# Spectral filter and feed-forward kernel: rows normalised ahead of the first stage, W mirrored by a gather, the row mean kept out of the residual, the d-transform cut by lo positions, and a new table of the order

## Chip, cores and metric

One core of a Trainium2 chip. The metric is the device time of one execution in microseconds (us). The engines are TensorE (PE; PEld is its weight load), VectorE (DVE), ScalarE (ACT), GpSimd (POOL) and SyncE (SP, which here only issues transfers).

## The reference

Two rounds of a spectral block A and a feed-forward block B on x of 2048 positions (s) by 448 features (d), bf16:

```python
def _A_ref(x, w_r, w_i):
    X = rfft2(x.astype(float32), axes=(-2, -1))
    return irfft2(X * (w_r + 1j * w_i), (S, D), axes=(-2, -1)).astype(bfloat16)

def _B_ref(x, w1, b1, w2, b2):
    h = einsum("bsd,df->bsf", x, w1) + b1
    r = where(h > 0, h, 0)
    return einsum("bsf,fd->bsd", r * r, w2) + b2

x = x + _A_ref(_layernorm(x), A_w_r, A_w_i)
x = x + _B_ref(_layernorm(x), B_w1, B_b1, B_w2, B_b2)
x = x + _A_ref(_layernorm(x), A_w_r, A_w_i)
x = x + _B_ref(_layernorm(x), B_w1, B_b1, B_w2, B_b2)
```

S is 2048, D 448, the hidden width 1792; w_r and w_i have 2048 x 225 entries. The layernorm has no weights, only a mean and a standard deviation of each row.

## The kernel before

**Tiles.** x lies in SBUF as 16 tiles (t) of 128 rows. The transform over s is split: partition and tile give 16 coarse positions (hi) and 128 fine ones (lo). Frequencies go in pairs p = 1 to 7 and a special item p = 0.

**Spectral block.** Stage A (`first_A`, L803, and `second_A`, L1175) transforms over hi, tile by tile, into `XA`. Stage TD (`stage_TD`, L860) transforms over d into `U`, two components for each pair. Stage B (`stage_B`, L877) transforms over lo with the constants `G_sb` into `EF`. Stage W (`stage_W`, L910) multiplies by the filter on DVE: each pair needs rows of W and their mirror image. Stage Bi (L949) goes back over lo (matmuls with `H_sb` or `HS_sb`) into `VT`, TI (L980) back over d into `TIo`, AI (L994) back over hi, with the residual added on DVE (L1030). In the first round stage A takes `xin` and a reversed copy `xr` as weights, matrix `FA` scaled by the row's 1/std (`Fs`, made on POOL), and a further matmul with `m2`, minus twice the row mean. The mirror image of W is made by matmuls with the reversal matrix `J_sb` (`w_mirror`, L761).

**Feed-forward block.** `ln_B` (L1049) makes the statistics: the residual operation sums a row on DVE as it writes, ACT sums its squares, DVE forms the variance (`u`), ACT takes the root. Tiles 0 to 3 are not normalised: their mean and std go as extra columns through the first product, against column sums of W1 that `w1_aux` (L743) makes by matmuls and small transfers. Tiles 0 and 1 are transposed on TensorE (`flip`, L1036), the others by DMA transposes on SP. Then `h_part` or `h_pairs` (first product; a relu on ACT, a square on DVE), then `o_tile` (second product; the residual on DVE, with `xb` = x + b2 ready beforehand). Behind each `o_tile` of the first round, DVE makes the statistics and sums for the second spectral block, tile by tile (tags A2.t).

**Order.** `_Sched` records all operations and then places them: at each step it takes, among the units that may start, by priority: the length of the chain behind a unit plus a bias out of `PR` and a table `ADJ` by tag. It also chooses between ACT and DVE for evacuations, picks the PSUM banks, and puts warm-up matmuls (`ones`, L1278) where it expects TensorE to be idle. Each engine then runs its list in order and waits on semaphores.

Of the kernel before, what the change touches and what calls it, by code (L numbers as in the profile page):

```python
# [10 lines left out]
P = 128  # L11
S = 2048
# [3 lines left out]
NFS = 6  # L16
NT = 16
# [8 lines left out]
H_PAIRS = tuple(p for p in range(1, 8) if p not in SD_PAIRS)  # L26

# [9 lines left out]
def make_constants():  # L37
# [20 lines left out]
    dd = np.arange(HD)[:, None]  # L58
    l = np.arange(1, 225)[None, :]
    th = 2 * np.pi * l * (dd - 223.5) / D  # L60
    TD = np.zeros((2, 2, P, LW))
    for g, M in enumerate((np.cos(th), -np.sin(th))):
        TD[g, 0] = M[:P]
        TD[g, 1, 32:] = M[P:]
# [11 lines left out]
    lo = (m % 8) * 16 + m // 8  # L76
    k2 = np.arange(P)
    kk = [0, 8, 1, 2, 3, 4, 5, 6, 7]
    G = np.zeros((P, 9, 3, P))
    H = np.zeros((P, 9, 2, 2 * P))  # L80
    for i, k1 in enumerate(kk):
        th = 2 * np.pi * lo[:, None] * (k1 + 16 * k2[None, :]) / float(S)
        G[:, i, 0] = np.cos(th)
        G[:, i, 1] = -np.sin(th)
        G[:, i, 2] = np.sin(th)
# [16 lines left out]
    for g, M in enumerate((cl * np.cos(th), cl * np.sin(th))):  # L102
        for r in range(2):
            TI[:, r, g] = M[r::2]

    HS = np.stack([np.stack([-H[:, p + 1, 1], H[:, p + 1, 0], H[:, p + 1, 1], -H[:, p + 1, 0]], 1) for p in range(1, 8)], 1)
# [5 lines left out]

PR = {'A1': 65800.0, 'A1step': 7500.0, 'TD': [48800.0, -113100.0], 'B': [36300.0, -23900.0], 'W': [76300.0, 35800.0], 'Bi': [21700.0, 28400.0], 'step': [16400.0, 1100.0], 'M': 33500.0, 'aux': -104400.0, 'ramp': [210200.0, 192900.0], 'rstep': [2800.0, 6700.0], 'late': [85200.0, 100700.0], 'lstep': [5400.0, 6200.0], 'TI': [53500.0, 42800.0], 'AI': [44600.0, 400.0], 'h': [57700.0, -6500.0], 'A2': -27100.0, 'xb': 113100.0}
ADJ = {"": -1463273, "A1.0": 1085981, "A1.1": 710040, "A1.2": 717802, "A1.3": 364623, "A1.4": 440691, "A1.5": 740255,
# [68 lines left out]
class _Unit:  # L183


    def __init__(self, eng, rows=128):
        self.eng = eng
        self.ops = []
        self.tiles = []
        self.rows = rows  # L190
        self.prio = 0.0
        self.bias = 0.0
        self.seq = 0
        self.tag = ""
# [1162 lines left out]
```

## Time and profile before

| what | us |
|---|---|
| runs, median of 3 (lowest, highest) | 273.26 (272.47, 273.49) |
| profiled execution, span | 271.4 |
| first matmul of stage A starts | 9.12 |
| last matmul of the first Bi ends (about) | 44.8 |
| first feed-forward's first h matmul starts | 52.29 |
| second d-transform starts | 148.16 |
| second feed-forward's first h matmul starts | 178.32 |
| last matmul ends | 268.9 |

The span goes from the first to the last instruction of the profiled execution; the runs are timed from outside, so what lies around the span is in their time and not in it. The page gives no time of its own for the profiled execution besides the span.

In the profile's rows "out<-in" names what an operation writes and reads. A row of the timeline begins with its start and its length in us; "[0.71 <-DVE ...]" behind it is idle time of the engine just before, and who ended it. Most matmuls have the one line L622 and most DVE operations L676, those of helper functions, so the names tell them apart: `Fs,tmp` is the second stage A, `TD_sb,XA` the d-transform, `arena,G_sb` stage B, `HS_sb` and `H_sb` stage Bi, `TI_sb,VT` and `tmp,FI_sb` the way back, `J_sb,x_sb` the flips, `yT,W_sb` and `yT,VT` the first product, `W_sb,arena` the second.

### The profile page before, as it was taken

How to read it: one execution, taken by the hardware profiler on the slowest of the kernel's cores; microseconds unless marked ns; L12 is line 12 of the kernel's file. 1: busy time of each engine (PE TensorE's matmuls, PEld its weight loads, DVE VectorE, ACT ScalarE, POOL GpSimd, SP SyncE). 2: the span in 40 equal slices, each digit the busy share in tenths (PEclk: the TensorE clock that was granted, in tenths of full speed). 3: DMA queues.
4: the chain of work that ended last, by engine and by line, in shares of the span. 5: the costliest groups of instructions: out<-in, count | busy, mean ns of one | idle time of the engine just before them, and what ended most of it. 6: DMA issues, size and time to landing. Idle time of an engine off the chain costs nothing.

```text
span 271.4 us, 5706 instructions
## 1 busy us (share of the span) xinstructions
PE 260.9 (96%) x2086; PEld 159.0 (59%) x2086; DVE 206.8 (76%) x730; ACT 179.4 (66%) x382; POOL 13.3 (5%) x28
## 2 busy tenths in 40 slices
PE   7899988999999999999998999988999999999996
PEld 2588736786744554445557775776764454454554
DVE  4878994999999999457996998398998654556122
ACT  2698986997849728786206897897667833787000
POOL 4860000000000000000000000000000000000000
DMA  7999800004203123000000000004242023200101
GB/s 254 341 382 304 215 14 2 2 4 77 61 14 41 32 46 70 2 1 2 0 0 2 2 0 1 2 1 42 56 97 68 0 66 81 41 0 2 51 34 51
DMA packets 28566, 16.71 MB, mean 62 GB/s; under 512 B 21838, under 2 KB 27194, under 8 KB 28412
## 3 DMA queue, kind: packets, MB, share of 16 engines
q1 hardware_dynamic: 28108, 15.62, 22.5%
q10 hardware_dynamic: 432, 0.75, 0.8%
q8 instruction: 16, 0.26, 0.4%
q14 instruction: 10, 0.08, 0.1%
HBM read 10.85 MB, written 1.84 MB: 47 GB/s over the span
## 4 chain that ended last, share of the span: by engine, by line
PE 77%; DVE 13%; DMA 3%; ACT 3%; issue 2%; POOL 0%; ACTq 0%; DVEq 0%
PE ps L622 77%; DVE tmp L676 6%; DVE arena L676 3%; DMA yT<-x_sb 2%; DVE st L777 1%; ACT tmp L647 1%; DMA xin<-in_A_x_dram 1%; ACT VT L1054 1%; ACT VT L647 0%; DVE VT L676 0%; DVE x_sb L1171 0%; PE ps L1278 0%; ACT mv L641 0%; DVE yT L648 0%; DVE Fs L659 0%
## 5 line engine op out<-in xcount | busy, mean ns | idle before, releaser
L622 PE MATMUL ps<-yT,W_sb 64*128 64x512 bf16 (+1 forms) x770 | 89.5, 346 | 1.0 <-DMA yT<-x_sb 0.7
L622 PE MATMUL ps<-W_sb,arena 128*128 128x448 bf16 (+1 forms) x476 | 86.6, 341 | 0.0
L622 PEld LDWEIGHTS ps<-yT,W_sb 64*128 64x128 bf16 (+1 forms) x770 | 50.6, 95 | 38.6 <-DMA yT<-x_sb 1.1
L622 PEld LDWEIGHTS ps<-W_sb,arena 128*128 128x128 bf16 x476 | 46.2, 98 | 37.3 <-DVE arena L676 0.4
L676 DVE TENSOR_TENSOR arena<-arena 128x512 bf16<-128x512 bf16 (+1 forms) x140 | 49.5, 369 | 21.9 <-ACT arena L641 21.6
L641 ACT ACTIVATE arena<-ps,b1col 128x512 bf16<-128x512 f32 x84 | 52.5, 686 | 12.8 <-PE ps L622 12.6
L1171 DVE SCALAR_TENSOR_TENSOR x_sb<-ps,arena 128x448 bf16<-128x448 f32 (+1 forms) x26 | 15.3, 587 | 17.3 <-PE ps L622 16.8
L647 ACT ACTIVATE arena<-ps 128x896 bf16<-128x896 f32 (+1 forms) x37 | 24.8, 784 | 2.2 <-PE ps L622 2.1
L641 ACT ACTIVATE mv<-mv,epst 128x2 f32<-128x2 f32 (+1 forms) x38 | 11.1, 295 | 20.8 <-DVE mv L778 15.7
L647 ACT ACTIVATE XA<-ps 128x512 bf16<-128x512 f32 x32 | 17.8, 603 | 6.7 <-PE ps L622 6.7
L641 ACT ACTIVATE arena<-ps 128x256 bf16<-128x256 f32 x56 | 19.1, 406 | 4.4 <-PE ps L622 3.4
L647 ACT ACTIVATE VT<-ps 128x512 bf16<-128x512 f32 (+1 forms) x32 | 17.9, 626 | 5.0 <-PE ps L622 5.0
L1054 ACT ACTIVATE VT<-x_sb 128x448 bf16<-128x448 bf16 x32 | 18.4, 580 | 3.8 <-DVE x_sb L1030 3.8
L622 PE MATMUL ps<-yT,VT 64*128 64x512 bf16 x42 | 15.8, 376 | 0.0
L622 PE MATMUL ps<-HS_sb,arena 128*128 128x512 bf16 x64 | 14.9, 380 | 0.7 <-DVE arena L676 0.6
L647 ACT ACTIVATE tmp<-ps 128x896 bf16<-128x896 f32 (+1 forms) x18 | 14.0, 849 | 2.2 <-PE ps L622 2.2
L668 ACT ACTIVATE arena<-x_sb,mv,rstd 128x448 bf16<-128x448 bf16 x11 | 8.3, 759 | 10.4 <-DMA yT<-arena 7.8
L622 PE MATMUL ps<-arena,G_sb 128*128 128x448 bf16 (+1 forms) x72 | 13.6, 332 | 0.0
L622 PE MATMUL ps<-TD_sb,XA 112*128 112x112 bf16 (+1 forms) x184 | 13.4, 229 | 0.0
L622 PEld LDWEIGHTS ps<-TD_sb,XA 112*128 112x128 bf16 (+1 forms) x184 | 12.2, 98 | 1.6 <-ACT XA L647 0.5
L676 DVE TENSOR_TENSOR VT<-tmp 128x448 bf16<-128x448 bf16 x24 | 8.8, 384 | 4.4 <-ACT tmp L647 4.4
L1030 DVE SCALAR_TENSOR_TENSOR x_sb<-ps,xin 128x448 bf16<-128x448 f32 x16 | 9.5, 620 | 3.3 <-PE ps L622 3.3
(81 smaller groups left out, 309.2 us busy)
## 6 DMA issues: line engine op xcount, KB each, us to landing
out_dram<-x_sb SPq DMA_DIRECT2D x15, 112.0 KB, 1.7
W_sb<-in_B_w_dram SPq DMA_DIRECT2D x1, 1568.0 KB, 15.6
W_sb<-in_B_w_dram SPq DMA_DIRECT2D x1, 1344.0 KB, 11.6
HS_sb<-c_HS SPq DMA_DIRECT2D x1, 1024.0 KB, 6.2
xin<-in_A_x_dram SPq DMA_DIRECT2D x2, 448.0 KB, 6.1
G_sb<-c_G SPq DMA_DIRECT2D x1, 672.0 KB
xin<-in_A_x_dram ACTq DMA_DIRECT2D x1, 448.0 KB, 6.0
yT<-in_A_w_r_dram SPq DMA_DIRECT2D x1, 392.0 KB
```

The source lines that it names most:

```text
L622: return sch.add("pe", lambda e: e.matmul(_res(o), lhsT, rhs, start=start, stop=stop, skip_group_check=skip), [lhsT, rhs], [o], cost=cost, ...
L641: sch.add("act", lambda e: e.activation(o, _res(i), func, **kw), rd, [o], cost=c)
L647: op = sch.add(engs[0], lambda e: e.activation(o, _res(i), ACT.Copy) if h[0].eng == "act" else e.tensor_copy(o, _res(i)), [i], [o], cost=c ...
L668: op = sch.add(engs[0], lambda e: e.activation(o, i, ACT.Identity, bias=b, scale=s) if h[0].eng == "act" else e.tensor_scalar(o, i, s, b, ...
L676: sch.add(eng, lambda e: e.tensor_tensor(o, _res(a), b, op), [a, b], [o], cost=_free(o) / rate + 69.0)
L777: small(lambda e, si=si, xi=xi: e.bn_stats(si, xi), [xi], [si], _free(xi) / 0.96 + 69.0)
L1030: small(lambda e, xx=xx, xi=xi, r=r, i=i: e.scalar_tensor_tensor(out=xx, in0=_res(r), scalar=1.0, in1=xi, op0=ALU.mult, op1=ALU.add, accum ...
L1054: sch.add("act", lambda e, i=i, o=o, x=x: e.activation(o, x, ACT.Square, accum_out=sd[:, i, 1:2]), [x], [o, sd[:, i, 1:2]], cost=560.0)
L1171: small(lambda e: e.scalar_tensor_tensor(out=o, in0=_res(i), scalar=r[0] if r else 1.0, in1=xb[:, t, d0:d1], op0=ALU.mult, op1=ALU.add), [ ...
```

## The change

1. **First stage A.** POOL (twelve tiles) or DVE (four) write the normalised row into `x_sb`, (x - mean) x 1/std in one operation, and the matmuls take it with the constant FA: four per tile in place of five. `Fs`, `xr` and `m2` are gone from this stage. The sums of tiles 1 and 3 are made on ACT. Statistics go in groups of one or two tiles.
2. **Mirrored W.** Two indirect transfers on POOL gather W's rows in reversed order into `Wm`, and POOL copies the 14 pieces that are wanted into `Wt`. The `J_sb` matmuls with their evacuations are gone.
3. **Row mean.** The residual behind the spectral block subtracts the row mean (`scalar=m`), so the row that the feed-forward normalises has mean zero: no row sum, and no variance steps on DVE. `xb` of the last round adds both means back, one operation per tile. `w1_aux` is gone.
4. **d-transform by halves.** A new order of columns in `XA` puts tiles 0 to 7 on even lo positions and 8 to 15 on odd ones. For each pair `TD_half` transforms one half of the lo positions, both components in one bank; in the second round as two 64-column halves of the array, 112 columns each. In the first round pair 1 takes eight matmuls in stage B in place of four, and DVE's two combinations for it go.
5. **Inverse d-transform of tiles 0 to 3** (`stage_TI4`) in one unit: the first halves of all four tiles, then the second halves, with four evacuations.
6. **Order.** `PR` and `ADJ` are replaced by `ORDER`: for each tag the place of each unit in one sequence, with a letter for the engine (a ACT, d DVE, p POOL). `schedule` goes through that sequence; only banks and warm-up matmuls are still chosen by estimates. Dependencies are kept for 2-byte in place of 4-byte places.

```diff
-PR = {'A1': 65800.0, 'A1step': 7500.0, ...
-ADJ = {"": -1463273, "A1.0": 1085981, ...
+ORDER = {
+    "TD0.0": "147 148a 141 145d", "B0.0": "154 157d 155 156a", ...
...
+        for i, w in enumerate((A_w_r, A_w_i)):
+            gather(Wm[:, i, :], w.rearrange("(p k) l -> p (k l)", k=16), back[:, 0:1])
...
+                evac(Wp[:, p, 3 - 2 * i, :], Wm[:, i, :].rearrange("p (k l) -> p k l", k=16)[:, 15 - p, 1:225], ["pool"])
...
-            for i in range(4):
-                    mm(q[lambda b, i=i: ps[32 * i:32 * i + 32, b, 0:D]], ones[:, 0:32], W1_sb[:, blk, D * i:D * (i + 1)],
...
-            dst = XA[:, :, :, :, 8 * t:8 * t + 8].rearrange("p k g c j -> p (k g) c j")
+            m = 16 * (t % 8) + t // 8
+            dst = XA[:, :, :, :, m:m + 15:2].rearrange("p k g c j -> p (k g) c j")
...
-            scaled(f, FA_sb[:], rstd[:, t, 0:1], EV["FS"])
+            xh, m, r = x_sb[:, t, 0:D], mv[:, t, 0:1], rstd[:, t, 0:1]
+            norm(xh, xin[:, t, :], m, r, EV["XH"])
...
+        def TD_half(q, p, hf, first):
+            lo = slice(hf, P, 2)
...
+            u = sch.new_unit("pe", 64)
+            for n in range(8):
+                for e in range(2):
+                    g, x, c, m = parts[e][n // 2]
+                    r = n % 2
+                    l0 = g * 256 + r * QD
+                    mm(q[lambda b, l0=l0, e=e: ps[64 * e:64 * e + 64, b, l0:l0 + QD]], x(r, c), TQ_sb[:, m, r, :],
+                       n == 0, n == 7, skip=True, unit=u)
...
+        def stage_TI4():
+            q = [_Tile(1) for _ in range(4)]
+            u = sch.new_unit("pe")
+            for r in range(2):
+                for t in range(4):
+                    for g in range(2):
+                        mm(q[t][lambda b, g=g: ps[:, b, g * HD:(g + 1) * HD]], VT[0:QD, r, g, t].rearrange("p c j -> p (c j)"),
+                           TI_sb[:, r, g, :], r == 0 and g == 0, r == 1 and g == 1, skip=True, unit=u)
...
-                    out=xx, in0=_res(r), scalar=1.0, in1=xi, op0=ALU.mult, op1=ALU.add, accum_out=sd[:, t + i, 0:1]),
+                    out=xx, in0=_res(r), scalar=m, in1=xi, op0=ALU.subtract, op1=ALU.add), [r, xi, m], [xx], 536.0)
```

What the order becomes, at three places. First POOL at the kernel's start. In the rows of before `VT` is the reversed copy xr, `Fs` the scaled FA:

```order
L689 MEMSET arena 128x32x32
L689 MEMSET ones 128x128
L689 MEMSET x_sb 128x16x64
L648 COPY VT<-xin 128x448 x2
L648 COPY VT<-xin 128x896
L659 ISA
L659 TENSOR_SCALAR Fs<-FA_sb,rstd 128x256 x6
L648 COPY VT<-xin 128x896
L659 TENSOR_SCALAR Fs<-FA_sb,rstd 128x256 x4
```

and now, with the gathers (`DMA yT<-...,back`), the normalised rows (`x_sb<-xin,mv,rstd`) and the copies of mirrored W (`Wt<-yT`):

```order
L704 MEMSET ones 128x128
L726 ISA
L726 IOTA back 128x1
L699 DMA yT<-in_A_w_i_dram,back 128x3600
L699 DMA yT<-in_A_w_r_dram,back 128x3600
L676 TENSOR_SCALAR x_sb<-xin,mv,rstd 128x448
L704 MEMSET x_sb 128x16x64
L676 TENSOR_SCALAR x_sb<-xin,mv,rstd 128x448 x9
L657 COPY Wt<-yT 128x224
L676 TENSOR_SCALAR x_sb<-xin,mv,rstd 128x448 x2
L657 COPY Wt<-yT 128x224 x13
```

The gathers' issues and a memset now stand around the first normalised row, and POOL makes rows of 448 where it made columns of 256.

Second, TensorE between the two rounds: the end of the first feed-forward and the start of the second d-transform, before

```order
L622 MATMUL ps<-Fs,tmp 128x128 x4
L622 MATMUL ps<-W_sb,arena 128x224 x14
L622 MATMUL ps<-Fs,tmp 128x128 x20
L1278 MATMUL ps<-ones 128x512 x2
L622 MATMUL ps<-Fs,tmp 128x128 x4
L1278 MATMUL ps<-ones 128x512 x4
L1278 MATMUL ps<-ones 128x128
L622 MATMUL ps<-TD_sb,XA 128x112 x32
L622 MATMUL ps<-arena,G_sb 128x448 x4
```

and now:

```order
L631 MATMUL ps<-Fs,tmp 128x128 x12
L631 MATMUL ps<-W_sb,arena 128x224 x14
L631 MATMUL ps<-Fs,tmp 128x128 x16
L631 MATMUL ps<-TD_sb,XA 64x112 x64
L631 MATMUL ps<-Fs,tmp 128x128 x4
L631 MATMUL ps<-TD_sb,XA 64x112 x80
L631 MATMUL ps<-arena,G_sb 128x448 x4
```

64 half-width d-transform matmuls stand ahead of the last tile's stage A, where two warm-up matmuls stood, and no warm-up matmul is left behind it.

Third, ACT in the second ramp, from the last `VT` evacuation of Bi to the first relu, before (`tmp` is TIo, `VT,mv<-x_sb` the sum of squares, `mv<-mv` the root):

```order
L647 ACTIVATE VT<-ps 128x32x16 x2
L647 ACTIVATE tmp<-ps 128x448 x2
L647 ACTIVATE tmp<-ps 128x896 x3
L1054 ACTIVATE VT,mv<-x_sb 128x4x112 x2
L641 ACTIVATE mv<-mv 128x1 x2
L647 ACTIVATE tmp<-ps 128x896 x2
L1054 ACTIVATE VT,mv<-x_sb 128x4x112
```

and now:

```order
L656 ACTIVATE VT<-ps 128x32x16
L656 ACTIVATE tmp<-ps 128x448 x4
L656 ACTIVATE tmp<-ps 128x896
L1108 ACTIVATE VT,mv<-x_sb 128x4x112 x2
L650 ACTIVATE mv<-mv,epst 128x1 x2
L656 ACTIVATE tmp<-ps 128x896 x3
L1108 ACTIVATE VT,mv<-x_sb 128x4x112
```

Two 448 evacuations came in ahead of the squares, and two of 896 moved behind the roots.

More of the change, by code (lines that the diff above doesn't have):

```diff
@@ L371, in fits @@
[L371 to L385 removed]
+        rows = 128
@@ L479, in schedule @@
                 t += op.cost
+                free[e] = t
                 done[op] = t
@@ L488, in schedule @@
             if e == "pe":
-                used.append((start, t))
-            free[e] = t
-            for v in order[u]:
-                left[v] -= 1
-                if left[v] == 0:
-                    enter(v)
+                rows = u.rows
+                used.append((begin, free["pe"]))
         self.length = max(done.values())
@@ L918, in stage_W @@
                 wa, wb = w[:, :, 0:2, :], w[:, :, 2:4, :]
-                if not first and p0 in V_PAIRS:
+                if p0 in (VB_PAIRS if first else V_PAIRS):
                     T[0:2] = E, F
```

638 lines of the change are left out of this document (292 added, 346 removed), and 136 rows, old and new, of tables (ADJ, ORDER).

## The prediction

> **What bounds the kernel now.** I read the page's busy times first, then its chain, then windows cut at the places where TensorE stops.
>
> ```profile
> span 271.4 us, 5706 instructions
> PE 260.9 (96%) x2086; PEld 159.0 (59%) x2086; DVE 206.8 (76%) x730; ACT 179.4 (66%) x382; POOL 13.3 (5%) x28
> PE 77%; DVE 13%; DMA 3%; ACT 3%; issue 2%; POOL 0%; ACTq 0%; DVEq 0%
> ```
>
> TensorE (PE) is nearly always busy and makes 77% of the chain. The next view gives stretches: length, then busy us of PE, PEld, DVE, ACT, POOL, the clock, the DMA share and GB/s.
>
> ```profile
> 9.10:19.80 10.70, 10.44 (x95) 8.88 (x96) 8.04 (x33) 9.72 (x23) 8.49 (x17) 1.00 1.12 348
> 19.70:44.80 25.10, 24.38 (x183) 15.72 (x181) 22.95 (x53) 21.42 (x37) 0.00 (x0) 1.00 0.56 154
> 44.70:52.30 7.60, 6.53 (x79) 5.09 (x78) 4.61 (x23) 6.87 (x14) 0.00 (x0) 1.00 0.01 3
> 145.70:148.20 2.50, 1.79 (x13) 0.70 (x11) 1.11 (x8) 2.36 (x6) 0.00 (x0) 1.00 0.02 7
> 148.10:170.70 22.60, 22.60 (x223) 15.48 (x221) 18.89 (x42) 19.21 (x33) 0.00 (x0) 1.00 0.00 1
> 170.70:178.30 7.60, 6.08 (x77) 5.08 (x75) 4.41 (x22) 7.00 (x15) 0.00 (x0) 1.00 0.01 3
> 188.40:189.10 0.70, 0.02 (x1) 0.00 (x0) 0.56 (x4) 0.36 (x3) 0.00 (x0) 1.00 0.00 0
> 189.10:268.90 79.80, 79.75 (x590) 43.32 (x590) 46.66 (x142) 40.80 (x82) 0.00 (x0) 1.00 0.18 45
> ```
>
> From 189.1 us TensorE runs without a gap, and the change leaves that feed-forward work as it is: nothing is to be had there. The clock is 1.00 throughout. What can move: the start (to 44.8 us, where ACT, DVE and PE share the load), the two ramps into the feed-forward (7.6 us each), the gap at 145.7, and the hole at 188.4.
>
> **The change, part by part.** The sum is made against the profiled execution: span 271.4 us; the runs' median of 273.26 is 1.9 us longer, which I keep.
>
> *Start of the kernel: 0.0 by 23.2 us.*
>
> ```profile
> 9.12 0.27 PE L622 MATMUL ps<-Fs,xin 128*128 128x256 bf16 x1 [0.84 <-POOL Fs L659]
> L659 POOL TENSOR_SCALAR Fs<-FA_sb,rstd 128x256 bf16<-128x256 bf16 x16 | 7.4, 478 | 0.9 <-DVE m L785 0.7
> L648 POOL COPY VT<-xin 128x448 bf16<-128x448 bf16 x2 | 1.1, 558 | 1.8 <-DMA xin<-in_A_x_dram 1.8
> L648 POOL COPY VT<-xin 128x896 bf16<-128x896 bf16 x3 | 2.8, 931 | 1.3 <-DMA xin<-in_A_x_dram 1.3
> 18.54 1.14 ACT L647 ACTIVATE XA<-ps 128x512 bf16<-128x512 f32 x2
> 34.77 0.94 PE L622 MATMUL ps<-W_sb,ones 128*32 128x448 bf16 x16
> ```
>
> Gone are 16 m2 and 14 J matmuls and the column sums (0.94 us, about paid back by four more 448-column matmuls for pair 1). But the stage is not TensorE's alone. POOL normalises 12 whole rows of 448; DVE takes four. No row shows that operation at 448: at least the 478 ns of 256 elements, at most in proportion, 478 x 448/256 = 837. The two copies grow by 373 ns per 448 elements, so I take 478 + 192 x 0.83 = 0.64 us, the nearer estimate. Tile 0's reciprocal stands behind the statistics of tiles 10 and 11, so its row is normalised at about 8.8; then the memset of x_sb (0.95), eleven rows and one copy: 8.8 + 0.95 + 11 x 0.64 + 0.35 = 17.1. ACT is later: two tiles' statistics push its first evacuation to about 9.8, and sixteen at 0.55 plus some six square roots at 0.2 end at 19.8, where the last one ends now (18.54 + 1.14 = 19.7). Two d-transform halves, two evacuations and the B matmuls then lead to the first W product at 23.2, as now (23.17 below). So TensorE's saving here stays behind ACT: 0, from -2.0 (ACT ahead, POOL's 17.1 decides) to +2.2 (837 ns on eleven rows).
>
> The two gathers stand ahead of every normalisation on POOL. Issuing one costs between 0.43 us (an issue of 128 rows on SP) and 7.24 (the dearest issue, 1792 tiny pieces):
>
> ```profile
> 2.12 0.43 SPq L614 DMA_DIRECT2D TD_sb<-c_TD  x1
> 18.49 7.24 SPq L614 DMA_DIRECT2D b1in<-in_B_b_dram  x1
> GB/s 254 341 382 304 215 14 2 2 4 77 61 14 41 32 46 70 2 1 2 0 0 2 2 0 1 2 1 42 56 97 68 0 66 81 41 0 2 51 34 51
> ```
>
> A gather has 128 rows, so I stay near the first: hidden, since POOL has nothing else to do before 8.8. The gathers also put 1.84 MB ahead of G and TD, while the DMA engines are full (share 1.12 from 9.1 to 19.8). By TD's end have then come x 1.84, FA 0.06, gathers 1.84, b2row 0.11, G 0.98 and TD 0.23 MB: 5.1 MB. The GB/s line above goes by slices of 6.8 us: 1.7 MB, 4.0, then 5.1 at 16.4 us. The first d-transform comes at about 18.5, so I take 0; no gain can come of it, and at half the rate for the gathers it costs 4.
>
> *Pair 1 skips two combinations: -0.7.*
>
> ```profile
> 23.17 0.68 DVE L676 TENSOR_TENSOR tmp<-arena 128x448 bf16<-128x448 bf16 x2
> 41.62 0.69 DVE L676 TENSOR_TENSOR arena<-tmp 128x448 bf16<-128x448 bf16 x2
> ```
>
> DVE works without a pause from 23.17 to 42.31 (22.95 us busy in that window); the last H and HS matmuls follow it. Without those two (0.68 us) all behind comes 0.7 earlier, if the mirrored W arrives: POOL has 13 copies left at 17.1, of 0.56 - 0.19 = 0.37 us each (half the elements of the 448 copy), to 21.9. At worst DVE waits for the last few: +2.
>
> The Trainium skill's page "SBUF — State Buffer", section "Who interferes with whom", says that a VectorE instruction with two SBUF inputs and a GpSimd one that reads SBUF block each other for a whole instruction. In this trace POOL stands still from 20 us, so no row shows the two together; by the rule a copy still open at 23.2 would stand against W products of 0.62, and five of them would make the -0.7 into some +1.
>
> *Between the layers: -1.5.*
>
> ```profile
> 144.79 0.93 PE L622 MATMUL ps<-Fs,tmp 128*128 128x128 bf16 x13
> 146.87 0.40 PE L622 MATMUL ps<-Fs,tmp 128*128 128x128 bf16 x4 [0.71 <-DVE tmp L685]
> 147.10 1.08 PE L1278 MATMUL ps<-ones 128*128 128x512 bf16 x5
> 148.16 1.73 PE L622 MATMUL ps<-TD_sb,XA 112*128 112x112 bf16 x32
> 149.73 0.92 PE L622 MATMUL ps<-arena,G_sb 128*128 128x448 bf16 x4
> 150.97 1.34 DVE L676 TENSOR_TENSOR tmp<-arena,Wt 128x448 bf16<-128x448 bf16 x4
> 156.84 0.62 DVE L648 CAST arena<-ps 128x448 bf16<-128x448 f32 x1
> 161.37 1.08 DVE L648 CAST arena<-ps 128x896 bf16<-128x896 f32 x1
> 167.19 0.69 DVE L676 TENSOR_TENSOR arena<-tmp 128x448 bf16<-128x448 bf16 x2
> ```
>
> From 145.7 to 148.16 TensorE does one tile's four matmuls (0.2) and otherwise warm-up or nothing: 2.2 us. After, 64 matmuls of the even lo positions, which need tiles 0 to 7 alone, stand before tile 15, and 32 more behind it: 96 halves, 96 x 25 ns = 2.4 us of work that fills the gap. What is late next is DVE: its W products run from 150.97 to 167.88 and would start only about 0.4 sooner; but two casts fall out of their stretch to ACT (0.62 and 1.08), and one VT cast comes in, so they end about 1.4 sooner. TensorE behind 148.16 has 22.6 - 2.4 = 20.2 us: 168.4, and ACT with 19.2 busy is as full. I take -1.5, between -0.4 (W chain alone) and -2.2 (the whole gap).
>
> *Ramps: -0.5 and -0.8; the hole: -0.7.*
>
> ```profile
> 169.68 1.03 PE L622 MATMUL ps<-HS_sb,arena 128*128 128x512 bf16 x4
> 171.90 3.41 ACT L647 ACTIVATE tmp<-ps 128x448 bf16<-128x448 f32 x5 [0.55 <-PE ps L622]
> 175.15 0.61 ACT L1054 ACTIVATE VT<-x_sb 128x448 bf16<-128x448 bf16 x1
> 177.72 0.27 PE L622 MATMUL ps<-J_sb,x_sb 128*128 128x128 bf16 x2 [0.35 <-ACT tmp L647]
> 178.32 6.29 PE L622 MATMUL ps<-yT,W_sb 128*128 128x256 bf16 x56 [0.33 <-DVE yT L648]
> 184.34 1.23 SPq L609 DMA_TRANSPOSE yT<-x_sb  x1
> 189.12 1.05 PE L622 MATMUL ps<-yT,W_sb 128*128 128x256 bf16 x8 [0.70 <-DMA yT<-x_sb]
> L676 DVE TENSOR_TENSOR arena<-x_sb,b2row 128x896 bf16<-128x896 bf16 x14 | 8.7, 618 | 0.0
> ```
>
> The path is the same: last VT, inverse d-transform, residual, squares, root, flip, first h. In the second ramp ACT does five evacuations (two of 448, three of 896: 3.41 us) before the first square; then it is four of 448 and one of 896, about 3.0: -0.4, and the 0.35 that the flip waited for ACT's bank goes too. In the first ramp one 896 evacuation (0.9) no longer parts the two roots, against 0.4 more ahead of the squares: -0.5. Each may give 0 to -1.3. The hole at 188.4 is the transpose of tiles 2 and 3, issued at 184.34, 4.7 us before it landed; without DVE's variance steps its root stands right behind the squares at the ramp's end, some 4 us sooner, so it hides: -0.7, at worst 0.
>
> In the late rows `xb` gets 16 vector operations of 448 in place of operations of 896 at 618 ns; if each costs as much as the residual's (0.6), that is 9.6 us for 4.9: DVE is busy 46.66 of 79.8 us there, so it is free; without that slack it would cost those 4.7. The removed accumulator reads and small steps relieve DVE where TensorE is full: 0.
>
> Sum: 0 - 0.7 - 1.5 - 0.5 - 0.8 - 0.7 = -4.2, span 267.2, time 267.2 + 1.9 = **269.1 us**.
>
> **Rivals.**
>
> *Half-width matmuls do not overlap.* 112-column matmuls now take 49 ns each (32 in 148.16 to 149.73). 224 halves at 49 are 11.0 us in place of 5.5. For overlap speaks the column-sum row: sixteen 32-column matmuls of 448 in 0.94 us, a quarter of their serial time. Against: no row shows an instruction pair below 49 ns. The stage would end at 145.7 + 0.2 + 22.4 + 5.5 = 173.8, that is 4.6 later than forecast: 273.7. The Trainium skill's page "TensorEngine Tiling (Array Packing)", sections "Key Properties" and "Restrictions", says that column tiling disables fast weight load and that a change of tiling mode drains TensorE; this rule would push the rate that way, and the 0.94 us row does not show it at 112 columns.
>
> *Slower: the gathers hold POOL.* POOL's queue is in order; two issues of up to 7.24 us from about 1.2 would set its first normalisation at 15.7 in place of 8.8, and everything behind 6.9 later: 276.0. Hidden until the two exceed 7.6 us together; slower than before from 11.8.
>
> *It does not do what it says:* W and ACT hold the second stage, the ramps keep their 7.6: only -0.7 - 0.4 - 0.7: 271.5.
>
> *More:* the start follows POOL's 17.1 and W begins 2 us sooner: 267.1.
>
> **How the numbers follow.** Forecast 0.44, more 0.16, does not do it 0.14, no overlap 0.12, gathers 0.14. A run tells about 0.5%, 1.4 us, from no change. Faster: 0.44 + 0.16 + half of 0.14 = 0.67; same: 0.07 + 0.12 = 0.19; slower 0.14. The range reaches from 265.5 (more, with the whole gap) to 274.0 (no overlap) and leaves out the gathers' case.
>
> **What would show it.** Right: no idle of TensorE before the last tile's four matmuls between the layers, first W product near 23, under 7.2 us from last HS to first h, no DMA wait behind the first h block. Wrong: POOL's first normalisation behind 10 us, waits of W products on POOL, half-width matmuls above 30 ns each, ACT idle in the start.

## The result, and the profile after

| | before | after |
|---|---|---|
| median of 4 runs (lowest, highest), us | 272.87 (272.36, 273.49) | 285.53 (285.35, 285.98) |
| ratio, 95% interval | | 1.0463 (1.044 to 1.0486) |
| span of the profiled execution, us | 271.4 | 283.6 |

The change makes the kernel 4.6% slower; the forecast was 1.5% faster. The spans differ by 12.2 us. Cut at the same landmarks (starts and ends from the timelines of TensorE and DVE), this is where they come from:

| stretch | before | after | difference | forecast |
|---|---|---|---|---|
| start to the first W product on DVE | 23.17 | 36.45 | +13.28 | 0 |
| from there to the end of the last HS matmul | 21.60 | 21.75 | +0.15 | -0.7 |
| ramp 0, to the first h matmul | 7.52 | 7.05 | -0.47 | -0.5 |
| first feed-forward, to the end of the second product | 92.28 | 93.75 | +1.47 | 0 |
| between the layers, to the end of the last HS matmul | 26.14 | 25.16 | -0.98 | -1.5 |
| ramp 1, to the first h matmul | 7.61 | 6.79 | -0.82 | -0.8 |
| second feed-forward, to the last matmul | 90.55 | 90.11 | -0.44 | -0.7 |
| sum | | | +12.19 | -4.2 |

The start is 13.28 us longer and the first feed-forward 1.47; the first ramp and the last three stretches give 2.71 back. The page of the changed kernel (the span, the busy times, POOL's slices, the granted clock's slices, the chain by engine):

```profile
span 283.6 us, 5727 instructions
PE 263.4 (93%) x2154; PEld 160.4 (57%) x2156; DVE 209.7 (74%) x669; ACT 177.9 (63%) x389; POOL 30.1 (11%) x35
POOL 3999900000000000000000000000000000000000
PEclk9875999999999999999999999999999999999999
PE 81%; POOL 5%; DMA 5%; ACT 4%; DVE 3%; issue 1%; SPq 0%; ACTq 0%; DVEq 0%
```

The first W product, which ends the start in the table, is this row of DVE's timeline:

```profile
36.45 0.69 DVE L683 TENSOR_TENSOR tmp<-arena,Wt 128x448 bf16<-128x448 bf16 x2
```

POOL was busy for 13.3 us and is now for 30.1, all of it before 35 us, and it has come into the chain with 5% (it had 0). DVE, 13% of the chain before, has 3%. POOL's own timeline says why (start, length, operation, count; idle before in brackets):

```profile
3.12 0.95 POOL L699 DMA_INDIRECT yT<-in_A_w_r_dram,back  x1 [0.30 <-issue]
7.43 1.86 POOL L676 TENSOR_SCALAR x_sb<-xin,mv,rstd 128x448 bf16<-128x448 bf16 x1 [3.35 <-DVE rstd L792]
9.24 0.94 POOL L704 MEMSET x_sb<- 128x1024 bf16 x1
10.18 16.58 POOL L676 TENSOR_SCALAR x_sb<-xin,mv,rstd 128x448 bf16<-128x448 bf16 x9
27.08 3.69 POOL L676 TENSOR_SCALAR x_sb<-xin,mv,rstd 128x448 bf16<-128x448 bf16 x2
30.73 4.15 POOL L657 COPY Wt<-yT 128x224 bf16<-128x224 bf16 x13
```

The gathers were issued in time and the first row began at 7.43, earlier than the 8.8 of the forecast. But a row takes 1.85 us, not 0.64: nine rows without a pause in 16.58, the twelfth done at 30.77 (17.1 in the forecast, with a copy). TensorE waits for nearly every one of them, and ACT waits for TensorE. Two more rows of that stretch, the first matmul of stage A and ACT's evacuation of XA (group, count, busy us, mean ns, idle before):

```profile
11.59 1.65 PE L631 MATMUL ps<-FA_sb,x_sb 128*128 128x256 bf16 x7 [5.19 <-DMA FA_sb<-c_FA]
L656 ACT ACTIVATE XA<-ps 128x512 bf16<-128x512 f32 x32 | 21.9, 743 | 19.4 <-PE ps L631 19.3
```

TensorE stood idle for 5.19 us before stage A's first matmul, until FA landed at 11.45 (before, FA landed at 8.41 and that matmul started at 9.12). And the evacuation that writes XA in the new order of columns takes 743 ns; before it was

```profile
L647 ACT ACTIVATE XA<-ps 128x512 bf16<-128x512 f32 x32 | 17.8, 603 | 6.7 <-PE ps L622 6.7
```

Between the layers, and the windows of the other stretches (length, then busy us of PE, PEld, DVE, ACT, POOL, clock, DMA share, GB/s):

```profile
160.14 1.76 PE L631 MATMUL ps<-TD_sb,XA 112*64 112x112 bf16 x64
162.31 0.38 PE L631 MATMUL ps<-Fs,tmp 128*128 128x128 bf16 x4 [0.40 <-DVE Fs L668]
162.62 2.37 PE L631 MATMUL ps<-TD_sb,XA 112*64 112x112 bf16 x80
```

```profile
11.50:33.50 22.00, 14.70 (x82) 8.53 (x83) 8.20 (x33) 12.26 (x22) 22.00 (x21) 0.69 0.92 301
36.40:58.20 21.80, 20.66 (x140) 13.21 (x140) 20.10 (x46) 18.84 (x34) 0.00 (x0) 1.00 0.11 39
58.10:65.30 7.20, 6.41 (x79) 5.10 (x78) 4.08 (x14) 6.47 (x16) 0.00 (x0) 1.00 0.00 0
166.00:184.20 18.20, 18.10 (x182) 11.28 (x179) 17.96 (x42) 14.89 (x29) 0.00 (x0) 1.00 0.01 2
191.00:281.10 90.10, 90.05 (x677) 54.63 (x676) 58.95 (x168) 49.91 (x115) 0.00 (x0) 1.00 0.21 42
```

From 11.5 to 33.5 POOL is busy the whole 22.00 us, TensorE two thirds of it, ACT a little over half and DVE less. The DMA engines are busy too (share 0.92), so that a crowded start stays a rival until the first experiment. 64 half-width matmuls take 1.76 us, 27.5 ns each, where a full-width one of 112 columns took 49 before: they overlap in pairs, and they fill the gap but for 0.40. The hole of 0.7 at the second feed-forward's start is gone.

### The profile page after: what moved, and what is told of

It is laid out like the page before. It is cut to its first block, busy times and chain, and to the rows that moved or that the text cites. A ratio compares the mean times of both kernels' runs of the same rounds, so it can differ in the third digit from the quotient of the medians.

```text
span 283.6 us, 5727 instructions
## 1 busy us (share of the span) xinstructions
PE 263.4 (93%) x2154; PEld 160.4 (57%) x2156; DVE 209.7 (74%) x669; ACT 177.9 (63%) x389; POOL 30.1 (11%) x35
## 4 chain that ended last, share of the span: by engine, by line
PE 81%; POOL 5%; DMA 5%; ACT 4%; DVE 3%; issue 1%; SPq 0%; ACTq 0%; DVEq 0%
PE ps L631 81%; POOL x_sb L676 5%; DMA xin<-in_A_x_dram 3%; ACT arena L656 2%; DMA yT<-arena 2%; ACT tmp L656 1%; DVE st L785 1%; DVE arena L683 1%; DVE x_sb L1084 0%; ACT VT L1108 0%; SPq L623 0%; DVE tmp L683 0%; ACT mv L650 0%; DVE x_sb L1204 0%; DVE mv L776 0%
## 5 line engine op out<-in xcount | busy, mean ns | idle before, releaser
L683 DVE TENSOR_TENSOR arena<-arena 128x512 bf16<-128x512 bf16 (+1 forms) x140 | 44.5, 363 | 14.6 <-ACT arena L650 14.5
L656 ACT ACTIVATE XA<-ps 128x512 bf16<-128x512 f32 x32 | 21.9, 743 | 19.4 <-PE ps L631 19.3
L656 ACT ACTIVATE arena<-ps 128x448 bf16<-128x448 f32 (+1 forms) x41 | 24.7, 725 | 3.8 <-PE ps L631 3.6
L631 PE MATMUL ps<-FA_sb,x_sb 128*128 128x256 bf16 x64 | 12.6, 353 | 12.4 <-POOL x_sb L676 7.2
L676 POOL TENSOR_SCALAR x_sb<-xin,mv,rstd 128x448 bf16<-128x448 bf16 x12 | 22.1, 1850 | 3.4 <-DVE rstd L792 3.4
L650 ACT ACTIVATE mv<-mv,epst 128x1 f32<-128x1 f32 (+1 forms) x44 | 12.1, 295 | 12.0 <-DVE mv L786 10.9
L631 PEld LDWEIGHTS ps<-FA_sb,x_sb 128*128 128x128 bf16 x64 | 6.6, 118 | 18.5 <-POOL x_sb L676 11.3
L656 ACT ACTIVATE VT<-ps 128x512 bf16<-128x512 f32 (+1 forms) x28 | 13.8, 556 | 4.9 <-PE ps L631 4.7
L631 PE MATMUL ps<-TD_sb,XA 112*64 112x112 bf16 (+2 forms) x296 | 13.8, 223 | 0.0
L1084 DVE SCALAR_TENSOR_TENSOR x_sb<-ps,mv,xin 128x448 bf16<-128x448 f32 x16 | 10.4, 677 | 4.2 <-PE ps L631 4.2
```

Of the source, the lines that this page charges most:

```text
L631: return sch.add("pe", lambda e: e.matmul(_res(o), lhsT, rhs, start=start, stop=stop, skip_group_check=skip), [lhsT, rhs], [o], cost=cost, ...
L650: sch.add("act", lambda e: e.activation(o, _res(i), func, **kw), rd, [o], cost=c)
L656: op = sch.add(engs[0], lambda e: e.activation(o, _res(i), ACT.Copy) if h[0].eng == "act" else e.tensor_copy(o, _res(i)), [i], [o], cost=c ...
L676: op = sch.add(engs[0], lambda e: e.tensor_scalar(o, i, m, r, op0=ALU.subtract, op1=ALU.mult), [i, m, r], [o], cost=c[engs[0]])
L683: sch.add(eng, lambda e: e.tensor_tensor(o, _res(a), b, op), [a, b], [o], cost=_free(o) / rate + 69.0)
L1084: small(lambda e, xx=xx, xi=xi, r=r, m=m: e.scalar_tensor_tensor(out=xx, in0=_res(r), scalar=m, in1=xi, op0=ALU.subtract, op1=ALU.add), [r ...
```

## The experiments

Theory 1: the subtraction makes a row dear on POOL, and the rows hold the start. Rivals: the start was crowded (DMA, DVE; theory 2 in e1), or x and FA came too late behind the gathers. Every ratio is against runs of the kernel before on the same chip.

| kernel | median us (runs) | ratio, 95% interval | span | first W product |
|---|---|---|---|---|
| after | 285.53 (4) | 1.0463 (1.044 to 1.0486) | 283.6 | 36.45 |
| e1_bench | 289.16 (1) | | 287.4 | 36.41 |
| e2_dve | 276.09 (4) | 1.0116 (1.0092 to 1.014) | 274.1 | 28.62 |
| e3_dve_fa | 275.89 (4) | 1.0104 (1.0078 to 1.0129) | 274.3 | 28.78 |
| e4_dve_fa_cont | 275.58 (4) | 1.0099 (1.0073 to 1.0124) | 273.8 | 27.57 |
| e5_add | 275.53 (4) | 1.0098 (1.007 to 1.0126) | 273.6 | 27.58 |
| e6_add_fa_cont | 271.61 (5) | 0.9941 (0.9922 to 0.996) | 269.9 | 24.20 |
| e7_add_fa_cont_gl | 274.46 (7) | 1.0045 (1.0029 to 1.0061) | 272.7 | 27.64 |
| e8_all | 274.38 (6) | 1.0054 (1.0028 to 1.0081) | 272.6 | 27.47 |
| e9_no_skip | 270.38 (4) | 0.9908 (0.9875 to 0.9942) | 268.5 | 24.09 |
| e10_no_fill | 273.99 (10) | 1.0042 (1.0018 to 1.0066) | 273.1 | 23.94 |
| e11_gather_2nd | 275.83 (5) | 1.0076 (1.0035 to 1.0117) | 274.0 | 28.51 |
| e12_fa_alone | 272.93 (1) | | 271.1 | 25.08 |
| e13_gl_clean | 271.66 (6) | 0.9949 (0.9932 to 0.9965) | 269.9 | 25.53 |

**e1_bench: what makes a row dear.**

```diff
+            px(lambda e: e.tensor_scalar(bo[:, 0:D], bi[:, 0:D], a, 1.0, op0=M_, op1=M_))
+            px(lambda e: e.tensor_scalar(bo[:, 0:D], bi[:, 0:D], a, b, op0=S_, op1=M_))
+            px(lambda e: e.tensor_scalar(bo[:, 0:D], bi[:, 0:D], a, b, op0=M_, op1=M_))
+            px(lambda e: e.tensor_scalar(bo[:, 0:D], bi[:, 0:D], a, 1.0, op0=S_, op1=M_))
+            px(lambda e: e.tensor_scalar(bo[:, 0:256], bi[:, 0:256], a, b, op0=S_, op1=M_))
+            px(lambda e: e.tensor_scalar(bo[:, 0:256], bi[:, 0:256], a, 1.0, op0=M_, op1=M_))
```

> The changed kernel with 36 more POOL operations on scratch data behind its own 14 copies of W (six of each of six forms; the output of the kernel is not touched). The question is why one normalised row (TENSOR_SCALAR, 128x448, subtract a per-row value and multiply by a per-row value) took 1.85 us on POOL where 0.64 was forecast. Theory 1, the form itself is dear: subtract-multiply with two per-row operands takes 1.8 to 1.9 us at 448 here too, with the DMA queues nearly quiet, and near 1.06 (1.85 x 256/448) at 256, while multiply by one per-row value takes 0.48 at 256 and 0.84 or less at 448. The form with a subtraction and one per-row operand, and that with two multiplications, tell which of the two is dear. Theory 2, the start of the kernel was crowded (transfers, VectorE): all forms at 448 take 0.84 or less here, and those beside a busy VectorE more than those beside an idle one.

The lines of the diff are L1311 to L1316 in their order. From POOL's timeline, a round beside DVE's residuals (63.97 on) and four rows of the stretch in which DVE makes its W products (36.4 to 58):

```profile
63.97 0.63 POOL L1311 TENSOR_SCALAR Fs<-xin,bs 128x448 bf16<-128x448 bf16 x1
64.71 1.85 POOL L1312 TENSOR_SCALAR Fs<-xin,bs 128x448 bf16<-128x448 bf16 x1
66.67 0.71 POOL L1313 TENSOR_SCALAR Fs<-xin,bs 128x448 bf16<-128x448 bf16 x1
67.47 1.78 POOL L1314 TENSOR_SCALAR Fs<-xin,bs 128x448 bf16<-128x448 bf16 x1
...
44.15 1.10 POOL L1311 TENSOR_SCALAR Fs<-xin,bs 128x448 bf16<-128x448 bf16 x1
45.35 2.31 POOL L1312 TENSOR_SCALAR Fs<-xin,bs 128x448 bf16<-128x448 bf16 x1
52.22 2.30 POOL L1315 TENSOR_SCALAR Fs<-xin,bs 128x256 bf16<-128x256 bf16 x1
54.62 1.04 POOL L1316 TENSOR_SCALAR Fs<-xin,bs 128x256 bf16<-128x256 bf16 x1
```

Two multiplications take 0.63 with one per-row operand and 0.71 with two; with a subtraction it is 1.78 and 1.85. So it is the subtraction, not the second operand, and it is dear with the DMA queues quiet too: theory 1. (At 256 elements the subtraction took 1.22 at the least, more than the 1.06 that was expected in proportion.) The crowding is real but another thing: beside the W products the 0.63 become 1.10 and the 256-wide multiplication (0.47 at best) 1.04. It goes both ways: the stretch from the first W product to the last HS matmul took 24.13 us here in place of 21.75. DVE's 448-wide products in the same window (36 to 55 us) of the kernel after and of this one show it:

```profile
L683 DVE TENSOR_TENSOR arena<-tmp 128x448 bf16<-128x448 bf16 x6 | 2.0, 383 | 0.0
```

```profile
L684 DVE TENSOR_TENSOR arena<-tmp 128x448 bf16<-128x448 bf16 x4 | 1.6, 467 | 0.0
```

**e2_dve, e3_dve_fa, e4_dve_fa_cont: the rows on DVE, then FA first, then XA without gaps.**

```diff
-    "A1.10": "15 19 14 16 22 26 61p 65 73 44p 46 54",
+    "A1.10": "15 19 14 16 22 26 26d 65 73 26d 46 54",
...
-        "277 3 530 10 0 9 6 1 5 38
+        "277 3 530 -1 0 9 6 1 5 2
...
-            m = 16 * (t % 8) + t // 8
-            dst = XA[:, :, :, :, m:m + 15:2]
+            dst = XA[:, :, :, :, 8 * t:8 * t + 8]
```

> The changed kernel with all sixteen normalised rows of the first stage on DVE (0.40 us each there), each right behind its reciprocal; POOL keeps the gathers and the copies. Theory, POOL's rows are the bound of the start: the stage then waits for FA (landed at 11.5) and ACT: 11.6 + 0.5 + 16 evacuations of 0.74 + some ten roots of 0.2 give a last XA evacuation near 26 in place of 33.4, the first W product near 29 in place of 36.45, and a span near 276. Rival, what holds the start is the arrival of x behind the gathers: the last XA evacuation stays behind 31 and the span above 281.

> As the run before, and FA's transfer is the first that ACT issues, ahead of two pieces of x. Theory, FA queued behind the gathers costs some 2.5 us: the first matmul at 8 to 9 in place of 11.6 and the span near 273.5. Rival, the pieces of x are late as well (x waits of 2 us on DVE) and hold the stage at the same place: the first matmul comes earlier but the first W product by less than 0.8, span 275 or more.

> As the run before, with XA's columns in an order that the evacuations write without gaps (tiles 0 to 7 in the first 64, 8 to 15 in the last 64); the d-transform then takes contiguous halves, in the first round as 64-column matmuls in pairs too; constants to suit, so the result is the reference's. Theory, writing every second element is what took the XA evacuation from 603 to 743 ns: it goes back to about 0.6, the start, where ACT is the bound by now, ends 16 x 0.14 = 2.2 earlier, and the stretch between the layers gains 0.5 to 1: span near 270.5. Rival, the evacuation stays at 0.74, or ACT isn't the bound: less than 1 us.

e2: the first W product at 28.62 (some 29 forecast) and a span of 274.1: the rows on POOL were the bound. The span gave 1.7 more than the start's 7.8, since the stall in the first feed-forward (below) isn't there. e3: the first matmul comes at 7.98, the first W product not earlier (28.78): what the rival said of the start, but not its cause, and the span (274.3) lies between the two. x isn't what holds it: with sixteen rows of 0.42 beside its statistics DVE is busy 15.47 of the 16.60 us from 6.2 to 22.8 and is the bound. e4 (with the constants and the d-transform's matmuls to suit): the evacuation's row goes back to

```profile
L656 ACT ACTIVATE XA<-ps 128x512 bf16<-128x512 f32 x32 | 16.9, 594 | 8.7 <-PE ps L631 8.7
```

so the gaps were its price, but the start gains 1.2, not 2.2, as DVE is still last there; between the layers it is 24.48 in place of 25.10. The profiled execution gave 1.2 back in its second feed-forward block (91.30 for 90.09), with two waits of TensorE that e3 doesn't have, and the medians of e3 and e4 don't differ by more than their intervals.

**e5_add: the rows on POOL, as an addition.** The decisive run: only the operation changes, and a tiny DVE operation turns the mean's sign.

```diff
-            op = sch.add(engs[0], lambda e: e.tensor_scalar(o, i, m, r, op0=ALU.subtract, op1=ALU.mult), ...
+            op = sch.add(engs[0], lambda e: e.tensor_scalar(o, i, m, r, op0=ALU.add, op1=ALU.mult), ...
...
+                sch.add("dve", lambda e: e.tensor_scalar(n, m, -1.0, 1.0, op0=ALU.mult, op1=ALU.mult), [m], [n], ...
```

> The changed kernel with one alteration: a normalised row is written as (x + (-mean)) x 1/std in place of (x - mean) x 1/std; the sign is turned by one tiny DVE operation behind each reciprocal. Engines, order and transfers are those of the changed kernel. Theory 1, it is the subtraction that is dear on POOL (1.78 us with it, 0.63 to 0.71 with two multiplications, DVE idle): a row then takes 0.63 to 0.75 us, POOL has all twelve rows done by some 18 us, the stage waits for FA (11.5) and ACT's sixteen evacuations of 0.74, first W product at 27.5 to 29, span 273 to 275. Theory 2, an addition is as dear as a subtraction on POOL: rows of 1.8, span near 283.6 as it was.

```profile
L676 POOL TENSOR_SCALAR x_sb<-xin,mv,rstd 128x448 bf16<-128x448 bf16 x12 | 8.5, 721 | 7.1 <-DVE mv L795 5.7 <-DVE mv L776 1.0 <-DVE mv L786 0.4
11.00 1.01 PE L631 MATMUL ps<-FA_sb,x_sb 128*128 128x256 bf16 x4 [3.83 <-DMA FA_sb<-c_FA]
```

(The first row is POOL's group, the second TensorE's timeline.) A row takes 0.72; POOL now waits for DVE, 7.1 us in all, and TensorE for POOL's rows hardly at all. The first W product comes at 27.58, 8.87 earlier, the span is 10.0 shorter: theory 1. What is left above the kernel before is 4.4 us of start, and FA's landing is one piece of it. The first W product's row:

```profile
27.58 0.69 DVE L683 TENSOR_TENSOR tmp<-arena,Wt 128x448 bf16<-128x448 bf16 x2
```

**e6_add_fa_cont.** e5 with FA first (the -1 of e3's edit; the other place in that line stays 38) and with XA's columns as in e4.

> As the run before, with FA's transfer ahead of x on ACT's queue and with XA's columns contiguous. Theory, with POOL out of the way the start is held by FA's landing and by ACT's evacuations (0.74 a piece with gaps, 0.6 without): first matmul near 8, sixteen evacuations with some ten roots end near 21.5, first W product near 24.5, between the layers another 0.6, span near 270. Rival, the late pieces of x (two to three us behind those of the kernel before, since the gathers share the DMA engines) hold it by DVE's statistics: first W product still behind 26.5, span 272 or more.

```profile
24.20 1.36 DVE L683 TENSOR_TENSOR tmp<-arena,Wt 128x448 bf16<-128x448 bf16 x4
```

First W product 24.20, last XA evacuation ended at 20.92, span 269.9: as the theory had it, and the first version that beats the kernel before, by 0.6%. With DVE relieved of twelve rows, FA's place and the gaps in XA are worth 3.4 us together. A third piece is in that sum: TensorE's granted clock was 0.50 from 9.6 to 16.4 us in e5, where FA came late, and 1.00 in e6. The gaps are probably the smaller part: e12 (below) still has them, with FA earlier and the clock at 1.00, and its first W product comes at 25.08.

**e7_add_fa_cont_gl, e11_gather_2nd, e13_gl_clean, e12_fa_alone: what the gathers cost.** In e7 the gathers wait for a piece of x; in e11 they stand behind POOL's first row; e13 is e9 (below) with that and all copies of W behind the last row; e12 is e5 with both, and with FA where the change has it. In these three the memset of x_sb's padding also moves behind the rows.

```diff
-            gather(Wm[:, i, :], ..., back[:, 0:1])
+            gather(Wm[:, i, :], ..., back[:, 0:1], [xin[:, 2, :]])
...
-                                                38 39 41 40 43 2 4
+                                                38 39 43 43 99 2 4
...
-    "M.6": "118 96"
+    "M.6": "118 102"
```

> As the run before, and the two gathers wait until the piece of x with tiles 2 and 3 has landed (some 3 us later than they were issued). Theory, the gathers' 1.84 MB take the DMA engines from x: x lands 1 to 2 us earlier, first W product 0.7 to 1.5 earlier than in the run before, span near 269. Rival, x isn't the bound, or the mirrored W now comes too late: first W product the same within 0.4, or W products that wait for POOL's copies and a span that is 0.5 longer or more.

> As e6, but the two gathers are issued behind POOL's first normalised row (at about 8.4 in place of 1.7) and the memset of x_sb's padding behind the rows. Theory, the gathers' traffic holds back x (the piece with tiles 2 and 3 landed 1.3 us earlier without it) and with it ACT's sums: first XA evacuation near 9.6 in place of 10.6, first W product near 23.4. Rival, the mirrored W then lands too late (12 us from issue to landing, 20 to 21, and 13 copies of 0.33 behind it): W products wait for POOL, and the last HS matmul comes 0.5 or more later than in e6.

> As the run with additions alone (e5, FA behind x on ACT's queue as in the changed kernel, landed 11.0), but both gathers are issued behind POOL's first normalised row and no copy of the mirrored W stands ahead of a row on POOL. The question is why FA, issued at 1.67 in both kernels, landed at 11.5 in the changed one and 8.5 before. Theory, the gathers' traffic: FA lands at 8 to 9 again and the first matmul starts at 8 to 9. Rival, SP's earlier large pieces (G at 2.8, behind it TD and FI) or the queue itself: FA still lands behind 10.

> As e9 (additions, FA first, contiguous XA, pair 1 with its two combinations on DVE; span 268.5, first XA evacuation 10.6, first W product 24.1), with the gathers behind POOL's first normalised row and every copy of W behind the last row. Theory, the gathers still cost the start something by the traffic that they put beside x and FA (FA landed 1.7 us earlier without them ahead of it): the start ends 0.5 to 1 earlier, first W product near 23.3, span near 267.7. Rival, with FA first nothing is left of that, and the later gathers only add a wait of POOL: first W product and span the same as in e9 within 0.4, or later.

One row of POOL of e7, e11 and e13 each, in this order, and TensorE's first of e12:

```profile
8.71 1.13 POOL L699 DMA_INDIRECT yT<-in_A_w_i_dram,back  x1 [7.61 <-DMA xin<-in_A_x_dram]
```

```profile
19.26 0.37 POOL L657 COPY Wt<-yT 128x224 bf16<-128x224 bf16 x1 [2.08 <-DMA yT<-in_A_w_i_dram,back]
```

```profile
11.21 6.29 POOL L676 TENSOR_SCALAR x_sb<-xin,mv,rstd 128x448 bf16<-128x448 bf16 x9
```

```profile
9.33 0.60 PE L631 MATMUL ps<-FA_sb,x_sb 128*128 128x256 bf16 x4 [3.21 <-DMA FA_sb<-c_FA]
```

e7 and e11 came out as neither theory nor rival: POOL's queue goes in order, and what waits in it holds the rows behind. In e7 the gather stood for x until 8.71 and the first row began at 11.12; in e11 one copy of W, ahead of the last two rows, stood 2.08 for a gather. e13, without that copy, is held up less but doesn't gain: its first W product comes at 25.53, 1.44 behind e9's, so the rival. The gathers' issues set POOL's second row to 11.21 in place of 9.41, and DVE's last two rows took 1.68 beside POOL's moved memset, in e9 0.79. Did x come earlier? DVE's second statistics started at 6.38 (in e9 at 6.08), so the first pieces didn't. The piece with tiles 8 to 11 landed at 7.96 in place of 9.16, but at 8.17 in e10, where the gathers stand ahead as in e9; the start gained nothing by it. So it isn't shown that the gathers' traffic holds x.

It probably holds FA where FA stands behind x. Stage A's first matmul waited for FA in each of these: it started at 9.33 in e12, against 11.00 in e5, from which e12 differs by the late gathers, and 10.13 to 11.59 in the four profiles with early gathers and FA in that place (after, e1, e2, e5). That is 0.8 to 2.3 us by one run, while no W product waited for a copy.

**e8_all: two rows of the first feed-forward on ACT.**

```diff
-"ln0.8": "479 439 481 482 485d 509d 527 531"
+"ln0.8": "479 439 481 482 485a 509a 527 531"
```

> As the run before, with the two normalised rows of tiles 8 and 9 in the first feed-forward block on ACT in place of DVE. In the profile of the changed kernel one of them stood 1.9 us on DVE for a transpose that landed 1.6 us late, with squares behind it that TensorE then waited for (0.27 and 0.94). Theory, that wait is a matter of a late landing and this order: with the rows on ACT no stall of TensorE over 0.2 us in the first feed-forward block, 92.2 us or less from the first h matmul to the end of the second product; where the run before has no such stall, the two are the same within 0.4. Rival, the stall has another source and shows here too.

Neither e7 nor e8 has the stall (92.12 and 92.19), so they are the same, and the question is left open by these two. What the changed kernel's profile shows of it, DVE and then TensorE:

```profile
83.33 0.34 DVE L668 TENSOR_SCALAR arena<-x_sb,rstd 128x448 bf16<-128x448 bf16 x1 [1.91 <-DMA yT<-arena]
```

```profile
84.83 0.55 PE L631 MATMUL ps<-W_sb,arena 128*128 128x448 bf16 x2 [0.28 <-DVE arena L683]
86.32 0.93 PE L631 MATMUL ps<-W_sb,arena 128*128 128x448 bf16 x4 [0.94 <-DVE arena L683]
```

The row on DVE waits for the transpose that still reads its buffer, the squares stand behind it, TensorE waits for those. That transpose took 4.6 us to land where those of e2 took 3.0 and 3.1. No profile of e2 to e13 has the stall in that place. The other profile with the subtraction on POOL, e1, has it: the transpose took 3.84 us there and TensorE stood still for 1.14 (its DVE is also slowed by POOL's extra operations).

What sets the late ones apart is in the DMA queues. From the issue to the landing of the 4.6 us transpose:

```profile
q1 hardware_dynamic: 1056, 0.26, 30.1%
q8 instruction: 1, 0.02, 1.4%
```

A transfer of instructions (queue q8, 16 KB, or q14, 8 KB) ran in that time. Over all 15 profiles, and all transposes whose landing they have, none of the 96 without such a transfer in its time took more than 3.17 us; of the 102 with one, 28 took over 3.3, up to 4.73, the others 3.0 to 3.3. So an instruction transfer goes with every late landing, though not every one makes a transpose late. That it is the cause wasn't tested.

**e9_no_skip: pair 1 as before.**

```diff
-VB_PAIRS = (1,)
+VB_PAIRS = ()
...
-    "W0.0": "159 161 158 160
+    "W0.0": "158 158 159 161 158 160
```

> As the run with additions, FA first and contiguous XA (e6, span 269.9, 21.9 us from the first W product to the last HS matmul), but pair 1 of the first round goes back to four matmuls in stage B and two combinations on DVE ahead of its products (0.68 us). Theory of the prediction, DVE's chain sets that stretch: it becomes 0.7 longer, 22.6 from DVE's first combination to the last HS matmul. Rival, TensorE has become as full as DVE there (in the changed kernel its HS matmuls ran without a pause from 50.3 to 56.5), and four matmuls fewer pay for the two combinations: the end of the last HS matmul moves by less than 0.3.

With its two combinations back on DVE the stretch is 21.43 in place of 21.91, and ramp 0 6.87 in place of 7.16. The rival, and more: skipping them costs 0.5, and e13 repeats it (21.45). In that stretch TensorE is busy 20.13 us in e9 and 20.77 in e6, DVE 20.36 and 20.09: the four matmuls add more to TensorE than the skip takes from DVE. e9 is the fastest kernel of the study, 0.9% ahead of the kernel before.

**e10_no_fill: the gap between the layers, empty again.**

```diff
-"TD1.0": "865 878d 884 885a"
+"TD1.0": "875 878d 884 885a"
```

(The same for TD1.2, TD1.4 and TD1.6.)

> As e6, but the 64 half-width d-transform matmuls that stand ahead of the last tile's stage A between the layers stand behind it, and warm-up matmuls fill the gap. Theory, what fills the gap is worth its whole length: 64 x 27 ns = 1.7 us more from the end of the second product to the last HS matmul, 26.2 in place of 24.5. Rival, DVE and ACT hold that stretch (DVE's casts follow the last tile's statistics without a pause): 0.3 to 0.8 more, under 25.3.

```profile
147.92 0.38 PE L631 MATMUL ps<-Fs,tmp 128*128 128x128 bf16 x4 [1.08 <-DVE Fs L668]
148.24 3.73 PE L631 MATMUL ps<-TD_sb,XA 112*64 112x112 bf16 x144
```

The stretch is 26.53 against 24.49: 2.04 more, beyond the 1.7 of the matmuls alone. The fill is worth its whole length; TensorE sets that stretch. The span is 3.2 longer than e6's, as the second feed-forward took 92.14 for 90.72: TensorE waits 0.33, 0.44 and 0.21 us in its first 28 us, where e6 has 0.36 alone; the rest of that 1.4 wasn't followed up.

## Why the prediction was wrong, step by step

**The step that failed** is the price of a normalised row on POOL: "at least the 478 ns of 256 elements, at most in proportion, 478 x 448/256 = 837". The bounds scaled the width of a row that was there (`Fs`, a multiplication) and took the form for granted; the operation has a subtraction where that row has a multiplication. The 0.64 fits the form it came from (0.63 in e1); with the subtraction the row takes 1.85, more than twice the upper bound. So the range from -2.0 to +2.2 for the start, and the step "TensorE's saving here stays behind ACT", fell with it: POOL's rows ended at 30.77, and POOL, not ACT, set the start. With the twelve rows at 0.72 (e5) 8.87 of the 13.28 us are gone. The rival that ended slower also looked to POOL, but to the gathers' issues; these took 1.16 and 0.95, hidden as forecast.

**The start, two smaller errors.** "By TD's end have then come ...: I take 0" summed what lands, and not the order in which it lands: FA, 64 KB behind two pieces of x, landed 3 us later (11.45 for 8.41), and the first matmul came 2.5 later; part of it goes with the early gathers (e12), the rest is open. And the new order of XA's columns was costed on TensorE alone, never on ACT, which writes them: 743 ns for 603, thirty-two times, which the sum had at 0.55 apiece for the first sixteen. In e6, with all three put right, the first W product comes at 24.20, 1.0 behind the forecast.

**Pair 1 (-0.7)**: wrong in sign. Before, DVE worked without a pause from 23.17 to 42.31, as the prediction says (19.14 of 19.14 us; its 22.95 is of the longer window 19.70:44.80), but TensorE was nearly as full (18.42), and in the changed kernel it is fuller than DVE (20.66 and 20.10 of 21.80 us in the window 36.40:58.20 above); e9 shows 0.5 lost by the skip. No W product waited for a copy: the copies ended at 34.9, the first product is at 36.45. The Trainium skill's page "SBUF — State Buffer", section "Who interferes with whom", has DVE with two SBUF inputs and a reading GpSimd block each other; e1 bears it out (0.63 to 1.10 on POOL, 383 to 467 ns on DVE), and it is by luck that the order of the changed kernel keeps them apart: the copies ended late, but the W products began later still.

**Between the layers (-1.5)**: the mechanism held (e10: 2.04). It gave 0.98 because the last tile's stage A ended 3.69 behind the second product, where it was 2.70. Without the gaps in XA that is 3.17 and the stretch 24.49, 1.65 gained, so half of the delay is ACT's evacuations of 0.74; the other half, with a root that stands behind six of them, is only seen in the trace. (The working counts 32 halves behind the last tile; the order and the trace have 80.) Half-width matmuls at 27.5 ns: that rival was wrong, and the rule that the prediction names from the Trainium skill's page "TensorEngine Tiling (Array Packing)" costs at most 3 ns a matmul here at 112 columns (27.5 against half of 49).

**Ramps (-0.5, -0.8)**: right in their sums, -0.47 and -0.82, with 6.79 to 6.81 in the second ramp of every kernel of the study and 7.05 to 7.18 in the first, but for e9 and e13 (6.87, 6.95). In the parts there is some luck. In the first ramp the way to ACT's first square grew by 0.06 (forecast 0.4) and the rest shrank by 0.54 (0.9). In the second nearly all, 0.74, came ahead of the first square, where ACT's evacuations went from 3.41 to 2.66 us (forecast 3.0), and 0.08 behind it, where 0.35 was expected.

**The hole (-0.7)**: gone in the changed kernel, 0.44 gained, but not for the reason given. The transpose is issued 3.8 us behind the first h matmul, where it was 6.0: 2.2 sooner, not 4. The matmuls that need it come sooner too (7.5 in place of 10.1, by the kernels in which they wait), so the time left for the landing went from 4.1 to 3.7 us. What changed is the landing: 4.73 us before, 3.40 in the changed kernel, a difference that the order wasn't meant to make. Where it took 3.9 to 4.0 (e5, e6, e10, e11, e12) a hole of 0.28 to 0.36 is back, in e6 for example:

```profile
184.52 0.72 PE L631 MATMUL ps<-yT,W_sb 128*128 128x256 bf16 x5 [0.36 <-DMA yT<-x_sb]
```

**The first feed-forward (0)** was costed as untouched, and in e2 to e13 it is (92.12 to 92.20, 92.28 before); the 1.47 of the changed kernel goes with a transpose that landed late, ahead of squares on DVE. The other three runs have no profile; their spans (283.6 to 284.2) are not shorter.

Of the signs of being wrong, "ACT idle in the start" was the one that came: of the 19.4 us before its XA evacuations in the row above 10.9 are in the start, 1.3 before the change. And of the signs of being right, "first W product near 23" failed.

The range's lower end doesn't follow from its terms: the rival with the earlier start, 267.1, with the whole gap (0.7 more than the forecast takes) gives 266.4, not 265.5.

## What to carry to other kernels

Scale a row of the trace to a new operation only if it is the same operation: another ALU function in the same instruction made it over two and a half times as long on one engine, while the neighbouring engine does it in 0.4 us. Bound an unseen form from above by something that has its function, or say that there is no upper bound, and give that case a chance. A new layout has two sides; cost the engine that writes it as well as the one that reads it. On an engine with one queue in order, an operation that waits for a transfer belongs behind all that others wait for.

## What the runs showed of the hardware

- On POOL a TENSOR_SCALAR of 448 bf16 took 0.63 (e1) to 0.72 us (e5) with a multiplication or an addition first, and 1.78 (e1) to 1.86 (the changed kernel) with a subtraction, where nothing disturbed it; x - m as x + (-m) is a gain of 1.1 us a row. DVE took 0.38 to 0.40 for the subtraction (the changed kernel).
- ACT's evacuation of 512 elements took 594 to 603 ns into runs of eight (e4, the kernel before) and 743 into every second element (the changed kernel).
- TensorE's granted clock was 0.50 from 11.5 to 14.9 and from 18.3 to 28.5 us of the changed kernel, and 1.00 between and behind; the 0.69 of the window above is the mean. Its 256-column matmuls of stage A took 370 to 421 ns in those two stretches and 272 to 283 outside. What that cost wasn't measured apart; POOL's rows, at 1.85 us whatever the clock, set the pace there.
- No transpose of 198 took over 3.17 us to land unless a transfer of instructions ran at the same time; with one, 28 took over 3.3, up to 4.73 us.
